# A weight pair in every second attention block, the queries' buffer as a thirteenth weight slot, and two of the eight w_out casts moved into attention

## The chip, the cores and the metric

One core of a Trainium2 chip runs the whole kernel. The metric is device time in microseconds (us). The engines are TensorE (PE in the profile, with its weight loads as PEld), VectorE (DVE), ScalarE (ACT), GpSimd (POOL) and SyncE (SP), whose instruction stream issues nearly all DMA transfers of this kernel. MB and GB/s are decimal; a transfer that the profile shows as 1024.0 KB is 1.049 MB.

## What is computed

The reference is three layers on float32 data, one behind the other:

```python
# 1. chunked attention: 4 batches, 8 heads, 768 tokens, 64 dims; chunks of 32 with 16 left, 8 right
k_full = concat([mem_k, k_ctx]); v_full = concat([mem_v, v_ctx])
scores = scale * (q_c @ k_full.T)
a = exp(scores - max); a = a / (sum(a) + 1e-9); out[:, :, c_start:c_end] = a @ v_full
# 2. soft mixture of experts on x (3072, 512): 8 experts of 4 slots, hidden 1024
logits = x @ phi
d = softmax over tokens; slot_input = d.T @ x
h = maximum(slot_input[e] @ w1[e], 0); slot_out[e] = h @ w2[e]
y = softmax over slots(logits) @ slot_out
# 3. a feed-forward layer on y (3072, 512), hidden 1024
h = y @ w_in; solu = h * softmax(h); ln = layer_norm(solu) * g_ln; result = ln @ w_out
```

`w_in` and `w_out` arrive as float64 (handed over as int64) and are turned into float32 on the chip.

## The kernel before

Every instruction's order is written out by hand. There are three phases.

**Attention**, a loop over 32 blocks (`GROUPS`, index g, lines 780 to 810). One block is a pair of heads, half a sequence, one batch. Per block PE does the score products (`emit_qk`, L245), DVE the softmax (L258 to L271), ACT the exponential and copies, PE a transpose and the value products (`emit_pv`, L292), and then transposes and products for the logits and the slot inputs (L303 to L354). Queries, keys and values come in transfers for two blocks: at an even g, SP issues the queries and keys that are used four blocks later (`load_q` L176, `load_k` L182, two transfers) and, behind `emit_pv(g - 1)`, the values used two blocks later (`load_v`, L182, two transfers). Each has two buffers, so SP holds an issue until PE has read the old content. SP works in order: what is queued behind a held issue waits as well.

In the same SP stream `load_e(LOADS[g])` issues weights ahead of their use. `LOADS` holds 2 at g = 1, 3, 5 of every eight blocks and 0 elsewhere; a 2 stands for 1.049 MB, which is one chunk of `w_in`, two chunks of `w_out`, or one unit of an expert's matrix. The list of what is loaded (`chunks`) is fixed: four times (a `w_in` chunk, two `w_out` chunks), then 32 expert units of 1.049 MB in the order of their use. The `w_out` chunks have places of their own; the others take the first free one of a list of slots. There are eight slots (tiles `e1`, `e2`, named `e_area` in the profile), and a `w_in` slot is freed during its cast. As attention ends, four buffers turn into slots: the two of the keys (`more("kz0")`, `more("kz1")`) and the two of the values; that makes twelve.

A **cast** of a 512-column half chunk (`cast_ops`) is in five steps, one step a block: ACT makes two float copies (L531, L532), DVE does the bits (L535; then L540 and L543), and `eng` multiplies and adds (L546, L549). All eight casts of `w_in` are in attention, with GpSimd as `eng`, starting at blocks `int(3 + 3.4 j)`: 3, 6, 9, 13, 16, 20, 23, 26. The eight casts of `w_out` are in the expert phase with DVE as `eng`, and have two more steps: ACT makes the high part (L566), DVE the low part (L570).

**Experts**, a loop over the 32 units (lines 857 to 874): PE multiplies with a unit (`emit_w1` L447, `emit_w2` L469), frees its slot, and `load_e()` issues the next unit into it (L222). A cast of `w_out` begins at every 2.6th unit (`LANE`), and the steps of the slot softmax (`combine`) run beside them.

**Tail**: 24 tiles of 128 tokens go through the feed-forward layer, planned by a list of times; its main products are L677.

Of the kernel before, what the change touches and what calls it, by code (L numbers as in the profile page):

```python
# [29 lines left out]
DM = H * D  # L30
KC = DM // P
E, SE, FF = 8, 4, 1024
NSLOT = E * SE
FC = FF // P
GT = 3
GROUPS = UNITS * 2
# [2 lines left out]
GREC = GCH + 1  # L39
GTOK = GT * P  # L40
NE = 24
CAST0, CASTN, NEARLY = 3, 3.4, 8
LOADS = [0, 2, 0, 2, 0, 2, 0, 0] * 4
LANE, SIDE = 2.6, 1

CASTU = (0, 1, 2, 3, 4, 5, 6)
C_ID, C_I4, C_REP, C_NM, C_PHI, C_G = 0, 128, 160, 288, 289, 417
# [24 lines left out]
def tile_kernel(ctx: ExitStack, tc: tile.TileContext, qr, kr, vr, w1, w2, w_in, w_out, cst, out):  # L72
# [11 lines left out]
    def area(tag, regions):  # L84

        total = 0
        for name, n in regions:
            total = (total + 31) // 32 * 32
            arenas[name] = [total, n, None]
            total += n  # L90
        tl = sb.tile([P, total], FP32, name=regions[0][0] + "_area", tag=tag)
        for name, _ in regions:
            arenas[name][2] = tl
# [3 lines left out]
    ])  # L97
    for i in range(3):
        area(f"x{i}", [(f"x{i}", GT * DM)])
    area("q", [("q", 4 * GTOK)])  # L100
    for i in range(2):
        area(f"kz{i}", [(f"kz{i}", 2048)])
        area(f"vz{i}", [(f"vz{i}", 4 * VS)])
# [6 lines left out]
    def at(name, off, n, dt=FP32):  # L110
        o, size, tl = arenas[name]
        assert off + n <= size, (name, off, n, size)
        v = tl[:, o + off:o + off + n]
        return v if dt == FP32 else v.bitcast(dt)
# [86 lines left out]
    slot_of = {}  # L201
# [354 lines left out]
        ops = cast_ops(raw(j), at("tmp", 512 * (t % 2), 512), w_in_f[:, sl], eng)  # L556
        return ops[:3] + [lambda: (ops[3](), release(("win", j // 2)) if j % 2 else None)] + ops[4:]

    def wout_ops(j, t):

        w = wo[t % len(wo)]

        def hi():
            area(f"w{j}", [(f"wh{j}", DM), (f"wl{j}", DM)])
            whi[j], wlo[j] = at(f"wh{j}", 0, DM, FP32R), at(f"wl{j}", 0, DM, FP32R)
            act.activation(out=whi[j], in_=w, func=ACTF.Copy, scale=g_sb[:, j:j + 1])  # L566

        return cast_ops(slot_of["wout", j], at("tmp", 512 * (t % 2), 512), w, dve) + [
            hi,
            lambda: dve.scalar_tensor_tensor(  # L570
                out=wlo[j], in0=w, scalar=g_sb[:, j:j + 1], in1=whi[j].bitcast(FP32), op0=ALU.mult, op1=ALU.subtract
            ),
        ]
# [178 lines left out]
    with tc.manual_schedule():  # L752
# [21 lines left out]
        casts = {}  # L774
        early = {}
        for j in range(NEARLY):
            for i in range(5):
                casts.setdefault(int(CAST0 + CASTN * j) + i, []).append((j, i))

        for g in range(GROUPS):  # L780
            if g + 1 < GROUPS:
                emit_qk(g + 1)
            emit_softmax(g + 1)
            if g == GROUPS - 4:
                more("kz0")
            if g == GROUPS - 2:
                more("kz1")
            if g % 2 == 0 and g + 4 < GROUPS:
                load_q(g // 2 + 2)
                load_k(g // 2 + 2)  # L790
            load_e(LOADS[g])
            if 1 <= g:
                emit_pv(g - 1)
            if g % 2 == 0 and 1 < g < GROUPS - 2:
                load_v(g // 2 + 1)
            if g == GROUPS - 2:
                more("vz0")
                load_e()
            for f, hb in todo.get(g, []):
                f(hb)  # L800
            if 3 <= g:
                emit_xt(g - 3)
            emit_t(g)
            emit_at(g)
            if g + 1 < GROUPS:
                emit_exp(g + 1)
            for j, i in casts.get(g, []):
                if j not in early:
                    early[j] = win_ops(j, j)
                early[j][i]()  # L810
        emit_softmax(GROUPS + 1)
        emit_dmax(HB - 2)
# [8 lines left out]
        emit_dt(HB - 2)  # L821
        if not TORD[0]:
            emit_xt(GROUPS - 1, 1)
        more("vz1")
        load_e()
        emit_lg(HB - 1, 3)
# [26 lines left out]
        after = []  # L853
        lane = []
        begun = 0
        waiting = [lambda t, j=j: wout_ops(j, t) for j in range(FC)]
        for n, u in enumerate(units):
            if u == units[-1]:
                keep_clock(bank(5), KEEP[0])
# [134 lines left out]
```

## Time and profile before

| | |
|---|---|
| median of 3 runs | 348.58 us (342.92 to 348.82) |
| the profiled execution | 346.0 us |
| its span in the profile | 344.2 us |
| PE busy | 305.1 us (89%) |
| DVE busy | 233.6 us (68%) |
| ACT busy | 212.4 us (62%) |
| POOL busy | 133.2 us (39%) |
| moved by DMA | 96.62 MB, mean 281 GB/s |

Busy shares are means over three phases with different limits. Attention lasts until about 126 us of the span, the experts until about 184 us, the tail until the end. Times below are microseconds from the span's start. A view by windows gives, for each stretch, what each engine was busy, the TensorE clock that was granted, and what the DMA engines moved.

### The profile page before, as it was taken

The numbers are of one execution on the slowest core, as the hardware profiler recorded it, in microseconds if no ns is written. First come the engines' busy times: TensorE is split into PE (matmuls) and PEld (weight loads), VectorE is DVE, ScalarE is ACT, GpSimd is POOL, SyncE is SP. The second block draws the span as 40 slices with busy tenths as digits, with TensorE's granted clock in tenths as the row PEclk, the third lists the DMA queues.
The fourth block names the chain that finished last, engine by engine and source line by source line (L and its number), as shares of the span: only waits on it lengthen the run. The fifth ranks groups of instructions, "written<-read, shape, count | busy, mean of one in ns | idle before, by whom it ended". The sixth has DMA issues, their size and how long they took to land.

```text
span 344.2 us, 7950 instructions
## 1 busy us (share of the span) xinstructions
PE 305.1 (89%) x3044; PEld 217.0 (63%) x3044; DVE 233.6 (68%) x418; ACT 212.4 (62%) x398; POOL 133.2 (39%) x301
## 2 busy tenths in 40 slices
PE   2796997988989989777757999999999999999996
PEld 2575665666666543332113678888888888888885
DVE  5386685877779359999100796879787878878540
ACT  1254646557566535765112588889888888888721
POOL 5002220231132023332100057777776767676610
PEclk9998999999999999898699999999999999999999
DMA  7989899999899999999990002576766665766631
GB/s 238 388 296 415 296 375 413 342 371 418 310 355 421 421 424 420 421 421 427 420 417 33 2 31 92 184 262 220 235 223 223 222 237 194 243 208 225 231 93 61
DMA packets 31942, 96.62 MB, mean 281 GB/s; under 512 B 4000, under 2 KB 14624, under 8 KB 27296
## 3 DMA queue, kind: packets, MB, share of 16 engines
q1 hardware_dynamic: 31760, 95.90, 74.0%
q8 instruction: 24, 0.39, 0.4%
q10 hardware_dynamic: 144, 0.22, 0.2%
q14 instruction: 14, 0.11, 0.1%
HBM read 79.32 MB, written 16.78 MB: 279 GB/s over the span
## 4 chain that ended last, share of the span: by engine, by line
PE 65%; DMA 23%; DVE 5%; ACT 4%; issue 2%; SPq 1%; ACTq 0%; DVEq 0%
PE bank L677 35%; DMA vz_area<-in_vr_dram 8%; DMA in_kz_area<-in_w_dram 6%; DMA in_vz_area<-in_w_dram 5%; PE bank L292 5%; PE bank L245 4%; DMA kz_area<-in_kr_dram 4%; PE h L589 3%; PE bank L303 2%; PE bank L311 2%; PE bank L317 2%; PE bank L282 2%; PE bank L354 1%; PE bank L447 1%; PE bank L687 1%
## 5 line engine op out<-in xcount | busy, mean ns | idle before, releaser
L677 PE MATMUL bank<-wh_area,yh_area 128*128 128x512 f32 x552 | 130.2, 391 | 0.0
L677 PEld LDWEIGHTS bank<-wh_area,yh_area 128*128 128x128 f32 x552 | 103.4, 188 | 22.1
L546 POOL TENSOR_TENSOR cst_area<-e_area,cst_area 128x512 f32<-128x512 f32 x8 | 10.4, 1305 | 83.1 <-DVE cst_area L258 62.3
L245 PE MATMUL bank<-kz_area,q_area 128*32 128x128 f32 x768 | 30.2, 295 | 10.3 <-DMA kz_area<-in_kr_dram 9.0
L292 PE MATMUL bank<-vz_area,s_area 128*32 128x130 f32 x768 | 29.8, 290 | 8.1 <-DMA vz_area<-in_vr_dram 4.9
L660 DVE STREAM_TRANSPOSE yv_area<-yq_area 128x1024 f32<-128x1024 f32 x20 | 24.9, 1245 | 17.3 <-DMA yq_area<-z 17.3
L604 DVE SCALAR_TENSOR_TENSOR eb_area<-h,eb_area 128x1024 f32<-128x1024 f32 x24 | 29.2, 1220 | 9.4 <-ACT eb_area L598 8.7
L263 DVE TENSOR_REDUCE cst_area<-bank 128x6 f32<-128x384 f32 x32 | 17.8, 557 | 25.9 <-PE bank L245 25.8
L595 DVE TENSOR_REDUCE cst_area<-h 128x1 f32<-128x1024 f32 x24 | 29.1, 1218 | 3.9 <-PE h L589 3.9
L642 POOL TENSOR_SCALAR cst_area<-cst_area 128x1 f32<-128x1 f32 x72 | 28.8, 399 | 7.7
L245 PEld LDWEIGHTS bank<-kz_area,q_area 128*32 128x32 f32 x768 | 21.0, 116 | 16.3 <-issue 6.2
L631 POOL TENSOR_SCALAR cst_area<-cst_area 128x1 f32<-128x1 f32 x24 | 18.5, 770 | 29.9 <-ACT eb_area L598 28.0
L292 PEld LDWEIGHTS bank<-vz_area,s_area 128*32 128x32 f32 x768 | 21.1, 114 | 13.0 <-ACT s_area L285 3.5
L598 ACT ACTIVATE eb_area<-h,cst_area 128x1024 f32<-128x1024 f32 x24 | 26.6, 1110 | 1.3 <-DVE cst_area L595 1.3
L627 ACT ACTIVATE eb_area<-eb_area,cst_area 128x1024 f32<-128x1024 f32 x24 | 27.3, 1139 | 0.1
L624 ACT ACTIVATE eb_area<-eb_area,cst_area 128x1024 f32<-128x1024 f32 x20 | 23.1, 1155 | 5.1 <-DVE eb_area L604 4.7
L671 DVE TENSOR_TENSOR yh_area<-yv_area,yh_area 128x1024 fp32r<-128x1024 f32 x20 | 24.5, 1223 | 2.3 <-ACT yh_area L667 2.3
L306 ACT COPY s_area<-bank 128x384 f32<-128x384 f32 x32 | 15.3, 477 | 15.1 <-PE bank L303 14.8
L667 ACT CAST yh_area<-yv_area 128x1024 fp32r<-128x1024 f32 x20 | 21.0, 1049 | 4.5 <-DVE yv_area L660 4.4
L643 POOL TENSOR_SCALAR cst_area<-cst_area 128x1 f32<-128x1 f32 x72 | 20.3, 283 | 7.1
L695 ACT ACTIVATE eb_area<-bank,cst_area 128x512 f32<-128x512 f32 x23 | 15.8, 686 | 10.3 <-POOL cst_area L633 7.4
L277 ACT ACTIVATE s_area<-s_area 128x384 f32<-128x384 f32 x32 | 16.9, 529 | 6.5 <-DVE s_area L268 6.5
(148 smaller groups left out, 501.3 us busy)
## 6 DMA issues: line engine op xcount, KB each, us to landing
e_area<-in_w_dram SPq DMA_DIRECT2D x23, 1024.0 KB, 13.8
vz_area<-in_vr_dram SPq DMA_DIRECT2D x32, 390.0 KB, 6.9
z<-eb_area SPq DMA_DIRECT2D x20, 512.0 KB, 2.8
yq_area<-z SPq DMA_DIRECT2D x80, 128.0 KB, 3.0
kz_area<-in_kr_dram SPq DMA_DIRECT2D x32, 232.0 KB, 6.3
q_area<-in_qr_dram SPq DMA_DIRECT2D x16, 384.0 KB, 6.3
out_dram<-eb_area SPq DMA_DIRECT2D x23, 256.0 KB, 2.1
in_kz_area<-in_w_dram SPq DMA_DIRECT2D x5, 1024.0 KB, 19.1
```

Of the source, the lines that this page charges most:

```text
L245: pe.matmul(out=bk[32 * j:32 * j + 32, t * 128:(t + 1) * 128], lhsT=qb[g // 2 % 2][:, GTOK * (g % 2) + c * CH:GTOK * (g % 2) + (c + 1) * C ...
L292: pe.matmul(out=bk[32 * j:32 * j + 32, t * 2 * VW:(t + 1) * 2 * VW], lhsT=atb[g % 2][:, c * CH:(c + 1) * CH], rhs=vz[g // 2 % 2][:, :, g % ...
L595: dve.tensor_reduce(out=sc("nm", i), in_=fin["h"][i % 2], axis=AX.X, op=ALU.max, negate=True)
L598: act.activation(out=eb[i % FIN], in_=fin["h"][i % 2], func=ACTF.Exp, bias=sc("nm", i), accum_out=sc("s", i))
L604: dve.scalar_tensor_tensor(out=ub[i % FIN], in0=fin["h"][i % 2], scalar=-1.0 / FF, in1=eb[i % FIN], op0=ALU.mult, op1=ALU.mult, accum_out= ...
L624: act.activation(out=yb[i % FIN], in_=ub[i % FIN], func=ACTF.Identity, scale=-float(FF), bias=sc("nu", i))
L627: act.activation(out=sq, in_=ub[i % FIN], func=ACTF.Square, scale=-float(FF), bias=sc("nu", i), accum_out=sc("vs", i))
L642: pool.tensor_scalar(out=t, in0=r, scalar1=r, scalar2=xx, op0=ALU.mult, op1=ALU.mult)
L660: dve.transpose(out=yv[i % FIN].rearrange("p (f a t) -> p a f t", f=FC, a=4), in_=yq[i % FIN].rearrange("p (a f t) -> p a f t", f=FC, a=4),)
L667: act.copy(out=yh[i % FIN][:, sl], in_=tps(i, sl) if i < NPE else yv[i % FIN])
L671: dve.tensor_tensor(out=yl[i % FIN][:, sl], in0=tps(i, sl) if i < NPE else yv[i % FIN], in1=yh[i % FIN][:, sl].bitcast(FP32), op=ALU.subtract,
L677: pe.matmul(out=fin["o"][i % 2], lhsT=a[i % FIN][:, f * 128:(f + 1) * 128], rhs=w[f], start=start, stop=stop)
```

## The change

The weight table gets its 2 in every odd block, also in g = 7, 15, 23 (and 31). The first block of each cast is given by a table. Two casts of `w_out` (chunks 0 and 1) join the eight of `w_in` in attention, in seven steps from blocks 17 and 24, with GpSimd as `eng`; their result stands in `wo0`, 512 new columns behind the queries' buffer. With these the queries' tile has the size of a slot, and as attention ends it becomes the thirteenth, `in_q`. In the expert phase six casts are left, one begun at every 3.4th unit.

```diff
-CAST0, CASTN, NEARLY = 3, 3.4, 8
-LOADS = [0, 2, 0, 2, 0, 2, 0, 0] * 4
-LANE, SIDE = 2.6, 1
+CASTS = (3, 5, 8, 10, 13, 16, 18, 21, 17, 24)
+NEARLY = len(CASTS)
+LOADS = [0, 2] * 16
+LANE, SIDE = 3.4, 1
...
-    area("q", [("q", 4 * GTOK)])
+    area("q", [("q", 4 * GTOK), ("wo0", DM)])
...
-    def wout_ops(j, t):
-        w = wo[t % len(wo)]
+    def wout_ops(j, t, w, eng=dve):
...
-        return cast_ops(slot_of["wout", j], at("tmp", 512 * (t % 2), 512), w, dve) + [
+        return cast_ops(slot_of["wout", j], at("tmp", 512 * (t % 2), 512), w, eng) + [
...
-            for i in range(5):
-                casts.setdefault(int(CAST0 + CASTN * j) + i, []).append((j, i))
+            for i in range(5 if j < 2 * KC else 7):
+                casts.setdefault(CASTS[j] + i, []).append((j, i))
...
-                    early[j] = win_ops(j, j)
+                    early[j] = win_ops(j, j) if j < 2 * KC else wout_ops(j - 2 * KC, j, at("wo0", 0, DM), pool)
...
+        more("q")
         more("vz1")
         load_e()
...
-        waiting = [lambda t, j=j: wout_ops(j, t) for j in range(FC)]
+        waiting = [lambda t, j=j: wout_ops(j, t, wo[t % len(wo)]) for j in range(NEARLY - 2 * KC, FC)]
```

The first place is on SP, in blocks 4 to 10 of attention (`q_area`, `kz_area`, `vz_area` are the buffers of queries, keys and values). Before, the queue read:

```order
L225 DMA e_area<-in_w_in_dram 128x1024
L176 DMA q_area<-in_qr_dram 128x768
L182 DMA kz_area<-in_kr_dram 64x928 x2
L182 DMA vz_area<-in_vr_dram 64x1560 x2
L176 DMA q_area<-in_qr_dram 128x768
L182 DMA kz_area<-in_kr_dram 64x928 x2
L182 DMA vz_area<-in_vr_dram 64x1560 x2
L225 DMA w_area<-in_w_out_dram 128x512 x2
```

Now it reads:

```order
L227 DMA e_area<-in_w_in_dram 128x1024
L178 DMA q_area<-in_qr_dram 128x768
L184 DMA kz_area<-in_kr_dram 64x928 x2
L184 DMA vz_area<-in_vr_dram 64x1560 x2
L227 DMA w_area<-in_w_out_dram 128x512 x2
L178 DMA q_area<-in_qr_dram 128x768
L184 DMA kz_area<-in_kr_dram 64x928 x2
L184 DMA vz_area<-in_vr_dram 64x1560 x2
```

The two chunks of `w_out` have moved from behind the values of block 8 to behind those of block 6; later weights follow suit, and expert units begin at block 17 in place of 21.

The second place is on SP where attention ends, from the last values (block 28) to the first slots that the expert phase fills again. Before:

```order
L182 DMA vz_area<-in_vr_dram 64x1560 x2
L222 DMA e_area<-in_w_dram 128x2048 x4
L222 DMA in_kz_area<-in_w_dram 128x2048
L222 DMA e_area<-in_w_dram 128x2048
L222 DMA in_kz_area<-in_w_dram 128x2048
L222 DMA in_vz_area<-in_w_dram 128x2048 x2
L222 DMA e_area<-in_w_dram 128x2048 x7
```

Now:

```order
L184 DMA vz_area<-in_vr_dram 64x1560 x2
L224 DMA e_area<-in_w_dram 128x2048 x2
L224 DMA in_kz_area<-in_w_dram 128x2048 x2
L224 DMA in_vz_area<-in_w_dram 128x2048
L224 DMA in_q_area<-in_w_dram 128x2048
L224 DMA in_vz_area<-in_w_dram 128x2048
L224 DMA e_area<-in_w_dram 128x2048 x8
```

Behind the last values nine units were issued before a slot had to be used twice; now there are seven, since six are issued ahead of the last values in place of three. After them 20 units were left, and now 19.

## Rows read from the trace of the kernel before

**Rows 1.** Page: the chain that ended last, shares of the span by engine.

```profile
PE 65%; DMA 23%; DVE 5%; ACT 4%; issue 2%; SPq 1%; ACTq 0%; DVEq 0%
```

**Rows 2.** Windows: stretch, engines' busy us (instructions), clock, DMA share, GB/s.

```profile
24.00:36.00 12.00, 8.60 (x161) 5.99 (x154) 7.02 (x20) 4.83 (x12) 2.58 (x2) 0.86 1.02 412
36.00:46.00 10.00, 9.61 (x218) 7.42 (x219) 7.96 (x22) 7.45 (x20) 2.59 (x2) 1.00 0.85 270
46.00:64.00 18.00, 16.01 (x307) 10.82 (x300) 12.55 (x35) 9.76 (x25) 3.00 (x3) 1.00 1.01 413
64.00:74.00 10.00, 9.06 (x191) 6.63 (x185) 8.26 (x25) 6.36 (x17) 4.13 (x4) 1.00 0.91 322
74.00:90.00 16.00, 14.04 (x263) 9.61 (x260) 11.28 (x33) 9.04 (x24) 3.19 (x3) 1.00 1.02 414
90.00:100.00 10.00, 8.89 (x206) 6.86 (x198) 8.65 (x25) 8.29 (x21) 2.58 (x2) 1.00 0.84 275
100.00:110.00 10.00, 9.95 (x201) 6.93 (x190) 7.62 (x23) 5.32 (x14) 2.58 (x2) 1.00 1.02 418
128.00:146.00 18.00, 14.95 (x174) 6.52 (x165) 17.34 (x32) 11.39 (x26) 6.55 (x7) 0.91 1.01 422
```

**Rows 3.** Timeline of SP in attention: start us, length, line, transfer, count.

```profile
29.32 1.14 SPq L182 DMA_DIRECT2D vz_area<-in_vr_dram  x2
37.13 0.33 SPq L176 DMA_DIRECT2D q_area<-in_qr_dram  x1
```

**Rows 4.** The chain in order of time, 140 to 184: start us, us, what.

```profile
144.65 18.59 DMA in_vz_area<-in_w_dram
...
163.29 19.73 DMA in_kz_area<-in_w_dram
...
183.07 1.06 PE bank L469 x8
```

**Rows 5.** Timeline of SP from the last values to the first refill.

```profile
104.36 1.11 SPq L182 DMA_DIRECT2D vz_area<-in_vr_dram  x2
...
128.06 6.93 SPq L222 DMA_DIRECT2D e_area<-in_w_dram  x7
```

**Rows 6.** Landing times: of those last values (L182, 104 to 106), then of all queries (L176).

```profile
DMA to landing us min/median/max: 5.1/5.3/5.5
...
DMA to landing us min/median/max: 2.9/6.3/8.5
```

**Rows 7.** The chain again: first expert product.

```profile
126.93 2.80 PE bank L447 x48
```

**Rows 8.** Groups by line: casts in attention, then of w_out (busy us, mean ns | idle before).

```profile
L531 ACT ACTIVATE cst_area<-e_area 128x512 f32<-128x512 f32 x8 | 5.5, 682 | 0.0
L532 ACT ACTIVATE e_area<-e_area 128x512 f32<-128x512 uint32 x8 | 5.4, 677 | 0.0
L540 DVE SCALAR_TENSOR_TENSOR cst_area<-e_area,cst_area 128x512 int32<-128x512 int32 x8 | 5.5, 682 | 0.0
L543 DVE TENSOR_SCALAR cst_area<-cst_area 128x512 int32<-128x512 int32 x10 | 4.5, 446 | 0.8
L535 DVE TENSOR_SCALAR cst_area<-cst_area 128x512 int32<-128x512 int32 x10 | 4.2, 417 | 0.0
L546 POOL TENSOR_TENSOR cst_area<-e_area,cst_area 128x512 f32<-128x512 f32 x8 | 10.4, 1305 | 83.1 <-DVE cst_area L258 62.3 <-ACT s_area L277 9.0 <-ACT s_area L306 6.0
L549 POOL TENSOR_TENSOR cst_area<-cst_area 128x512 f32<-128x512 f32 x8 | 10.2, 1277 | 0.6
L566 ACT ACTIVATE wh_area<-wo_area,cst_area 128x512 fp32r<-128x512 f32 x6 | 4.3, 722 | 5.4 <-DVE wo_area L549 5.4
L570 DVE SCALAR_TENSOR_TENSOR wh_area<-wo_area,cst_area,wh_area 128x512 fp32r<-128x512 f32 x6 | 4.5, 744 | 0.9 <-ACT wh_area L566 0.9
```

**Rows 9.** Page: issues of expert units into `e_area`: count, KB each, us to landing.

```profile
e_area<-in_w_dram SPq DMA_DIRECT2D x23, 1024.0 KB, 13.8
```

More of the change, by code (lines that the diff above doesn't have):

```diff
@@ L787, in tile_kernel @@
                 more("kz1")
+                assert max(casts) < GROUPS
             if g % 2 == 0 and g + 4 < GROUPS:
```

## The prediction

> **What bounds the kernel now.** I read the chain of work first: PE holds 65% of it and DMA 23% [rows 1]. In order of time it shows where the DMA part lies. From 144.65 to 183.02 the end is set by two weight loads in a row, 18.59 and 19.73 us, and then by the last expert product [rows 4]. So the expert phase ends when the stream of weights has run out, and whatever brings the last unit in earlier brings the tail earlier by as much. The tail itself is the same in both kernels.
>
> When is the stream out? A view by windows shows how full it is [rows 2]. There are two levels. From 24 to 36, 46 to 64 and 74 to 90 the core moves 412, 413 and 414 GB/s, in the expert phase 422. From 36 to 46, 64 to 74 and 90 to 100 it moves 270, 322 and 275 GB/s. The low stretches come once in eight blocks. The timeline of SP shows what precedes the first: the values of block 6 are issued at 29.32, block 7 has no weight pair, and SP issues nothing until PE has freed the queries' buffer at 37.13 [rows 3]. The loads under way run out, and the next two or three microseconds of issues meet an empty queue. The high stretches are those where each pair of blocks brings a weight pair; queries, keys and values are in them as well, so it is not the kind of transfer that makes the low rate.
>
> **The change part by part.** The baseline is the profiled execution, 346.0 us (span 344.2, and 1.8 around it). It lies 2.6 below the median of the three runs; the mean of these four executions is 346.6, and I state the forecast from that.
>
> *The pairs in blocks 7, 15 and 23.* Every later load moves up by up to three places, so three more expert units, 3 x 1.049 = 3.15 MB [rows 9], come ahead of the last values. The room: against 413 GB/s the three low stretches lack 143, 91 and 138 GB/s over 10 us each, together 3.72 MB [rows 2]. If the new pairs keep the queue from running dry, these stretches rise to 413. Filling all the room is worth 3.72 / 0.413 = 9.0 us, and the three units cost 3.15 / 0.413 = 7.6, so the last values land 1.4 us sooner. If only 3.15 MB of the room is used it is 0; if none, it is 3.15 / 0.370 = 8.5 us later (370 GB/s is the time-weighted mean of the seven windows from 24 to 110). I take -1.4, since the high stretches hold 413 for 18 us on end under the very pattern that the change makes general. PE can follow: it is busy 16.01 us of 18 in that stretch, and 9.95 of 10 where it is not held by loads.
>
> *The expert stream.* Behind the last values 26 units are left in place of 29. At 422 GB/s one takes 1.049 / 0.422 = 2.49 us [rows 2, 9], so three fewer give -7.5 us.
>
> *The hand-over, and the thirteenth slot.* The last values, issued from 104.36, the second transfer some 0.6 later, land 5.3 after that, at about 110.2 [rows 5, 6]. Behind them nine units fill the twelve slots, 9 x 2.49 = 22.4 us, until 132.6, and the first slot is filled again at 128.06 [rows 5]: the stream does not stop. Now only seven units are there, with `in_q` among them: they last 17.4 us. Moved by -1.4 the times are: last values 108.8, stream out at 126.2, first refill issued at 126.7. Until its data flow there is a start-up: 2.9 us is the shortest from issue to landing of 0.393 MB [rows 6], less 0.9 for moving it leaves 2.0, which includes the end of the transfer. So the start-up lies between 0 and 2.0, and the gap between 0.5 and 2.5. I take 1.8. Without `in_q` it would be one unit, 2.5 us, more. After the gap slots come free quicker than loads need them: PE did its first twelve units in 144.65 - 126.93 = 17.7 us, 1.5 each [rows 4, 7], against 2.49 for a load.
>
> *The casts.* One of w_out in attention costs ACT 0.68 + 0.68 + 0.72 = 2.1 us, DVE 0.42 + 0.68 + 0.45 + 0.74 = 2.3 and GpSimd 1.3 + 1.3 = 2.6 [rows 8]; two of them twice that, spread over blocks 17 to 30. I count nothing: in 74 to 90 ACT is busy 9.04 of 16 us and DVE 11.28 [rows 2], and what hides them is that PE waits for loads in every pair of blocks. Without that cover it is up to 2 x (2.1 + 2.3) = 8.8 us. Removing them from the expert phase takes at least 2 x 2.3 = 4.6 us off DVE, busy 17.34 of 18 there [rows 2], and gains nothing by itself, because the stream is what ends last; it only keeps DVE from being late when the phase gets shorter. The earlier starts of the w_in casts cost nothing either, as the chunks they read are also loaded earlier or at the same block.
>
> The sum: -1.4 - 7.5 + 1.8 = -7.1, so 338.9 against the profiled execution and 339.5 against the mean.
>
> One rule speaks against the first step. The Trainium skill (DMA: Bandwidth & Descriptors, Where 436 GB/s comes from) says that between HBM and SBUF the HBM side binds, at some 358 GB/s a core. By that attention would be full already at its mean and nothing could be filled in, which is the first rival below; the high stretches here, at 412 to 422, do not agree with it.
>
> **The rivals.**
>
> *The low stretches stay low on the average, because the queue is limited elsewhere than by missing weights.* Then attention pays 8.5 for the three units and the stream gives back 7.5, with the gap 1.8: +2.8, 349.4. For it: the stretch 90 to 100 stays at 275 although a pair stands in block 25; against it: that stretch begins with the drained queue, and 100 to 110 is back at 418 [rows 2].
>
> *The stream is filled, but PE reaches the expert phase no sooner.* The three units go into the room, and loads queued behind them make queries and values land later, or ACT and DVE are held by the casts near the end. Then the attention term is 0, and each microsecond that PE is late at the first refill lengthens the gap by one. With 0 to 2 us of that: 0 - 7.5 + 1.8 + (0 to 2) gives -5.7 to -3.7, 341 to 343.
>
> *The casts become the bound (slower).* If the 8.8 us of ACT and DVE work stand on the path of the blocks, the first refill comes 8.8 later and the stream stands still meanwhile: -7.1 + 8.8 = +1.7, 348.3. The break-even is 7.1 us of delay, and 2% slower needs 14, one and a half times what the rows give. For it: ACT work waits behind casts in order. Against it: the idle shares above. In a sentence beside it, the Trainium skill (SBUF — State Buffer, Who interferes with whom) says that a DVE instruction with two SBUF inputs and a GpSimd instruction that reads SBUF block each other; the four extra GpSimd instructions would then hold DVE up to 5.2 us, which no row here separates.
>
> *The change does nothing*, if the stream were not what ends last: [rows 4] exclude that for the expert phase. DVE could take over as the bound only if its work there did not shrink, and two of eight casts leave it.
>
> **How the numbers follow.** The forecast has 0.70, with its own range 336 to 342; the second rival 0.15, 341 to 343; the first 0.08, 349 to 351; the casts 0.07, 345 to 354. The predicted time is 339.5. The first two cases hold 0.85 between 336 and 343; with half a microsecond at the lower end for the start-up and three more at the upper one for the spread of single runs (342.92 to 348.82 before) the range is 335.5 to 346. A measurement of this kernel tells about 2% from no change; that bound is 341.6 from the median of the runs shown and 339.1 from the profiled execution. The forecast's middle lies between the two, so of its 0.70 I give 0.50 to faster, and the rest with the second rival and most of the others to the same: faster 0.50, same 0.43, slower 0.07.
>
> **What would show it.** Right, if the windows from 36 to 100 show 400 GB/s and more throughout, the last values land at about 109, the last unit's product starts at about 176 in place of 183.07, and DMA dips for about 2 us around 127. The first step is wrong if a stretch of 8 to 10 us under 330 GB/s is left between 36 and 100. The hand-over is wrong if the dip is over 4 us. The casts are wrong if the chain in attention runs through L531, L532 or L566 for more than a few microseconds, or GpSimd's L546 holds ACT. The forecast as a whole fails if the expert phase ends on something other than a load.

## The result and the profile after

The changed kernel takes 340.31 us in the median of six runs (338.71 to 341.21). The kernel before takes 346.38 in the median of six (342.92 to 350.06). The ratio is 0.9892, with a 95% interval from 0.9855 to 0.9929. It leaves out executions that are more than 1.5% above the fastest of their kernel, and so lies nearer to 1 than the ratio of the two medians, 0.9825. Over all 80 runs of the kernel before that were made beside these experiments the mean is 345.6; over ten of the changed kernel it is 340.7. So the gain is real: 1.1% or 3.7 us by the ratio (its interval says 2.4 to 5.0), 4.9 by the means of all runs. It stays inside 2%. The profiled execution takes 340.69, with a span of 338.9.

The chain that ended last, by engine (page of the changed kernel), with the same DMA share as before and 3 points less of PE [rows 1]:

```profile
PE 62%; DMA 23%; DVE 6%; ACT 5%; issue 1%; SPq 1%; ACTq 0%; DVEq 0%
```

The windows of the changed kernel (stretch, busy us and instructions of PE, PEld, DVE, ACT, POOL; granted clock, DMA share, GB/s), which answer [rows 2]:

```profile
24.00:110.00 86.00, 77.48 (x1488) 55.26 (x1488) 66.74 (x182) 54.85 (x138) 26.38 (x20) 0.98 1.02 404
36.00:46.00 10.00, 7.94 (x163) 5.86 (x166) 7.68 (x21) 7.40 (x18) 3.29 (x4) 1.00 1.00 394
64.00:74.00 10.00, 8.71 (x179) 5.97 (x177) 8.29 (x25) 8.51 (x21) 3.48 (x3) 1.00 1.02 413
90.00:100.00 10.00, 8.82 (x179) 6.56 (x178) 8.58 (x25) 6.38 (x17) 4.45 (x4) 1.00 1.00 390
...
126.00:130.00 4.00, 3.65 (x58) 1.75 (x54) 3.26 (x5) 2.56 (x7) 2.44 (x2) 1.00 0.59 178
128.00:146.00 18.00, 16.41 (x205) 7.40 (x201) 17.52 (x34) 11.80 (x28) 6.70 (x7) 1.00 0.98 406
```

The three low stretches are gone: 394, 413 and 390 GB/s stand where 270, 322 and 275 stood. In their place there is a short dip around 127: 178 GB/s from 126 to 130. It lies at the hand-over from attention to the expert phase, as the timeline of SP shows (start us, length, line, transfer, count; compare [rows 5]), with the landing time of the last values under it (compare [rows 6]):

```profile
103.38 1.11 SPq L184 DMA_DIRECT2D vz_area<-in_vr_dram  x2
...
115.44 0.33 SPq L224 DMA_DIRECT2D in_vz_area<-in_w_dram  x1
126.85 1.19 SPq L224 DMA_DIRECT2D e_area<-in_w_dram  x2
```

```profile
DMA to landing us min/median/max: 5.0/5.4/5.7
```

The last values are two transfers; the second, issued at 103.9, lands 5.7 later, at 109.6. Seven units are issued behind them, the last at 115.44, and then SP issues nothing until PE has freed the first slot at 126.85. Windows cut at that issue show where the dip lies:

```profile
125.00:126.85 1.85, 1.77 (x31) 1.19 (x34) 0.54 (x2) 1.18 (x3) 1.10 (x1) 1.00 0.49 208
126.85:129.00 2.15, 2.04 (x34) 0.96 (x26) 2.12 (x4) 0.71 (x3) 1.53 (x2) 1.00 0.55 99
129.00:130.00 1.00, 0.77 (x8) 0.29 (x12) 0.90 (x2) 1.00 (x4) 0.06 (x1) 1.00 0.98 410
```

The rate falls 1.85 us before the first refill is issued and is back 2.15 us behind the issue. Against 422 GB/s the first window lacks 0.9 us of the stream and the second 1.6, together 2.6.

The chain in order of time (start us, us, what; compare [rows 4]) still ends the expert phase on two loads and the last product:

```profile
139.41 18.51 DMA in_vz_area<-in_w_dram
...
157.99 19.72 DMA e_area<-in_w_dram
...
177.75 1.06 PE bank L471 x8
```

The last expert product starts at 177.75 in place of 183.07, 5.32 us sooner, and the whole execution is 346.0 - 340.69 = 5.31 shorter. So all of the gain is in hand by the last product, and the tail behind it adds nothing in this pair of traces.

### The profile page after: what moved, and what is told of

The parts are those of the page before. It is cut to its first block, busy times and chain, and to the rows that moved or that the text cites. A ratio compares the mean times of both kernels' runs of the same rounds, so it can differ in the third digit from the quotient of the medians.

```text
span 338.9 us, 7947 instructions
## 1 busy us (share of the span) xinstructions
PE 300.3 (89%) x3044; PEld 215.2 (63%) x3044; DVE 230.9 (68%) x414; ACT 212.4 (63%) x398; POOL 131.7 (39%) x305
## 4 chain that ended last, share of the span: by engine, by line
PE 62%; DMA 23%; DVE 6%; ACT 5%; issue 1%; SPq 1%; ACTq 0%; DVEq 0%
PE bank L678 36%; DMA vz_area<-in_vr_dram 9%; DMA e_area<-in_w_dram 6%; DMA in_vz_area<-in_w_dram 5%; PE bank L294 4%; DMA kz_area<-in_kr_dram 4%; PE h L590 4%; PE bank L247 3%; PE bank L305 2%; PE bank L313 2%; PE bank L319 2%; PE bank L356 1%; PE bank L284 1%; PE bank L449 1%; PE bank L688 1%
## 5 line engine op out<-in xcount | busy, mean ns | idle before, releaser
L294 PE MATMUL bank<-vz_area,s_area 128*32 128x130 f32 x768 | 28.8, 281 | 9.8 <-DVE cst_area L545 2.7
L294 PEld LDWEIGHTS bank<-vz_area,s_area 128*32 128x32 f32 x768 | 20.3, 110 | 14.9 <-ACT s_area L287 5.2
L643 POOL TENSOR_SCALAR cst_area<-cst_area 128x1 f32<-128x1 f32 x72 | 26.6, 369 | 7.7
L308 ACT COPY s_area<-bank 128x384 f32<-128x384 f32 x32 | 15.2, 476 | 18.7 <-PE bank L305 18.2
L644 POOL TENSOR_SCALAR cst_area<-cst_area 128x1 f32<-128x1 f32 x72 | 22.7, 315 | 7.1
L287 ACT COPY s_area<-bank 128x384 f32<-128x384 f32 x32 | 15.4, 480 | 4.7 <-PE bank L284 4.7
```

The costliest lines, as they stand in the source:

```text
L294: pe.matmul(out=bk[32 * j:32 * j + 32, t * 2 * VW:(t + 1) * 2 * VW], lhsT=atb[g % 2][:, c * CH:(c + 1) * CH], rhs=vz[g // 2 % 2][:, :, g % ...
L643: pool.tensor_scalar(out=t, in0=r, scalar1=r, scalar2=xx, op0=ALU.mult, op1=ALU.mult)
L644: pool.tensor_scalar(out=r, in0=t, scalar1=1.5, scalar2=r, op0=ALU.add, op1=ALU.mult)
```

## The experiments

The table holds what the runs gave, but for the two kernels of some 432 us, which have their place below. The means are those of all runs. "Landed" is when the second transfer of the last values of attention is in SBUF, "behind" the time from there to the start of the last expert product, both of the profiled execution. With 2.49 us a unit, 26 units take 64.7 us and 29 take 72.2. The experiments ran on four chips, and the kernel before took 345.2 us in the mean beside e1 to e4, 345.1 beside e5 to e7, 346.7 beside e8 to e10 and 346.3 beside e11, so a difference of a microsecond or so between means from two chips shows little.

| run | weight units behind the last values, slots | mean us (runs) | ratio, 95% interval | landed | behind | GB/s, 24 to 110 |
|---|---|---|---|---|---|---|
| kernel before | 29, 12 | 345.6 (80) | 1 | 110.4 | 72.6 | 371 |
| changed kernel | 26, 13 | 340.7 (10) | 0.9892 (0.9855 to 0.9929) | 109.6 | 68.1 | 404 |
| e9_changed_again | 26, 13 | 341.5 (4) | 0.9877 (0.9827 to 0.9928) | 110.2 | 67.9 | 409 |
| e1_loads_only | 26, 12 | 343.9 (10) | 0.9949 (0.9901 to 0.9997) | 110.0 | 71.1 | 412 |
| e2_no_q_slot | 26, 12 | 342.5 (10) | 0.9951 (0.9913 to 0.9989) | 107.6 | 70.9 | 414 |
| e3_old_loads | 29, 13 | 345.1 (10) | 0.9953 (0.9908 to 0.9997) | 107.0 | 72.8 | 378 |
| e4_casts_back | 26, 13 | 341.5 (10) | 0.9920 (0.9871 to 0.9969) | 109.9 | 67.9 | 411 |
| b2_before_again | 29, 12 | 348.8 (1) | none | 108.3 | 73.1 | 375 |
| e5_five_ahead | 27, 13 | 342.1 (10) | 0.9938 (0.9899 to 0.9977) | 108.5 | 71.3 | 396 |
| e6_keep_clock | 26, 13 | 341.0 (6) | 0.9905 (0.9864 to 0.9946) | 109.3 | 68.4 | 411 |
| e7_one_pair | 28, 12 | 343.8 (10) | 0.9986 (0.9955 to 1.0016) | 109.6 | 72.3 | 384 |
| e11_fourteen_apart | 26, 14 | 338.2 (6) | 0.978 (0.9698 to 0.9862) | 106.1 | 65.4 | 412 |

My theory was the prediction's: the expert phase ends when the stream of weights has run out, and the end is the moment of the last values, plus the units behind them, plus whatever time the stream stands still. Its rival was that attention pays for the three units or that PE comes later to the expert phase; the casts were a third suspect.

### One part at a time

The loads alone, on the kernel before:

```diff
-LOADS = [0, 2, 0, 2, 0, 2, 0, 0] * 4
+LOADS = [0, 2] * 16
```

> The kernel before with one edit: the weight pairs also in blocks 7, 15, 23 and 31. Twelve slots, all w_out casts in the expert phase. Stream theory (the end of the expert phase is the end of the weight stream): the windows 36-46, 64-74 and 90-100 rise from 270, 322, 275 to about 390 to 413 GB/s, as with the whole change; behind the last values (landing near 109.5) stand only 6 units, 14.9 us, so the stream stops near 124.5 and starts again near 128: a gap of 3.5 to 5 us in place of about 2. The last unit's product starts at about 180 (177.75 with the whole change, 183.07 before) and the time is about 343. Rival (the casts made the gain): the time stays with the kernel before, 346 or more. Rival (the slot made the gain): the same, 346.

The changed kernel without the queries' buffer as a slot:

```diff
-        more("q")
```

> The changed kernel without the thirteenth slot: the queries' buffer stays unused in the expert phase. Stream theory: one unit less behind the last values, so the gap at the hand-over near 127 grows by one unit's 2.49 us, the last product starts at about 180.2 in place of 177.75, and the time is about 342.8 in place of 340.3. Rival (twelve slots are enough, the gap is only a start-up time): no change, 340.3.

The changed kernel with the old pattern of loads:

```diff
-LOADS = [0, 2] * 16
+LOADS = [0, 2, 0, 2, 0, 2, 0, 0] * 4
```

> The changed kernel with the weight pairs of before (none in blocks 7, 15, 23), so with the slot and the casts alone. Stream theory: the three low stretches are back (near 270, 320, 280 GB/s), the hand-over has no gap since nine or ten units stand behind the last values, and the last product starts at 182 to 183; time 344 to 346. Rival (moving the casts, or the slot, made the gain): near 340 to 341.

Windows of the loads alone, cut at the first refill (issued at 127.74):

```profile
123.00:127.74 4.74, 4.41 (x43) 2.38 (x47) 1.79 (x6) 1.72 (x5) 1.11 (x1) 1.00 0.12 50
127.74:130.50 2.76, 2.41 (x38) 1.11 (x34) 2.55 (x5) 1.30 (x4) 1.58 (x2) 1.00 0.58 166
```

of the changed kernel without the slot (first refill issued at 125.13):

```profile
120.00:125.13 5.13, 4.64 (x46) 2.50 (x50) 2.11 (x7) 1.78 (x6) 1.10 (x1) 1.00 0.20 85
125.13:127.50 2.37, 2.04 (x34) 0.96 (x26) 2.34 (x4) 0.91 (x4) 1.59 (x2) 1.00 0.49 114
```

and of the changed kernel with the old loads, all of attention first:

```profile
24.00:110.00 86.00, 79.24 (x1530) 56.35 (x1530) 68.23 (x188) 55.74 (x140) 26.42 (x20) 0.98 0.98 378
36.00:46.00 10.00, 9.00 (x181) 6.13 (x175) 7.57 (x20) 7.69 (x20) 2.59 (x2) 1.00 1.01 366
...
90.00:100.00 10.00, 9.06 (x195) 6.35 (x183) 7.54 (x21) 6.67 (x18) 2.59 (x2) 1.00 1.00 384
...
126.00:130.00 4.00, 3.87 (x50) 1.66 (x54) 3.79 (x10) 3.12 (x8) 1.50 (x2) 1.00 1.02 430
```

The loads fill attention by themselves: 412 and 414 GB/s in both kernels that have them, 378 in the one that has the slot and the casts alone. With 12 slots, though, six units are left to issue behind the last values where the changed kernel has seven. The stream nearly stands still for some five microseconds before the first refill, at 50 and 85 GB/s, and comes back 2.8 and 2.4 us behind its issue. The time behind the last values is then 71.1 and 70.9 where the changed kernel has 68.1, and 72.6 before. So three microseconds of what the loads could bring are lost without the slot.

The slot without the loads, in turn, has no gap to fill: the stream does not stop (430 GB/s), and 72.6 stays 72.8. Its mean, 345.1, lies with that of the kernel before, and its ratio of 0.9953 says 1.6 us less. One part of what I expected there failed: the mean rate is that of the old loads again, but the three low stretches are not. They have 366, 375 and 384 GB/s in place of about 270, 320 and 280.

In the traces the two parts do not simply add: behind the last values the loads alone bring 1.5 us, the slot alone none, both together 4.5. The times do not separate this from a plain sum: by the ratios the parts bring 1.8 and 1.6 us and the whole 3.7 to 4.2, with intervals of a microsecond and more on each side.

### The casts

The two casts go back to the expert phase, where one is begun at every 2.6th unit again:

```diff
-CASTS = (3, 5, 8, 10, 13, 16, 18, 21, 17, 24)
+CASTS = (3, 5, 8, 10, 13, 16, 18, 21)
-LANE, SIDE = 3.4, 1
+LANE, SIDE = 2.6, 1
```

> The changed kernel with all eight w_out casts in the expert phase again (one begun at every 2.6th unit), weight pairs and thirteenth slot kept. Stream theory: the casts are worth nothing by themselves; the first refill comes up to 1 us sooner since DVE's L571 and ACT's copies leave the end of attention, DVE is busy again through 128 to 162, and the end is still the stream's: last product at 176.5 to 178, time 339 to 340.5. Rival (DVE would be the bound of the shorter expert phase): last product 180 or later, time 342.5 or more.

The mean is 341.5 against 340.7 of the changed kernel, a difference of 0.8 with an uncertainty of about as much. Landed and behind, 109.9 and 67.9, are those of the two traces of the changed kernel (109.6 and 110.2, 68.1 and 67.9). The other pair that differs by the casts, e1 and e2, shows 343.9 against 342.5 in the mean, but the same ratio, 0.9949 and 0.9951, and 71.1 and 70.9 behind. In no trace do the casts move the stream. If they are worth a microsecond it is in a place that I did not find, and that stays open. TensorE's clock is one place to look: its mean over the span is 0.977 in the ten runs of e4 and 0.984 in ten of the changed kernel, though 0.978 and 0.980 in e1 and e2. What they cost is bounded by the chain of the changed kernel in attention, in which these are all the pieces of casts from 36 to 112 (start us, us, line):

```profile
38.28 0.57 ACT cst_area L533
38.85 0.59 ACT e_area L534
...
44.28 0.56 ACT cst_area L533
44.84 0.57 ACT e_area L534
...
92.57 0.59 ACT q_area L533
93.16 0.59 ACT w_area L534
...
109.66 0.67 DVE wh_area L571
```

The first two pairs on ACT are casts of w_in. The third, whose result goes to `q_area`, where `wo0` lies, and the piece of 0.67 us on DVE belong to the moved casts of w_out: 1.85 us of the chain. The last values land no later for it (109.6 and 110.2 with these casts in attention, 109.9 without), so I see no cost; that there is none is not shown by one chain.

### The kernel before once more

> The kernel before, unedited, for a second trace. Theory: the low stretches of the load stream are a property of the order of the loads, so this trace shows them again at 36-46, 64-74 and 90-100, within 15 GB/s of 270, 322 and 275, the last values land at 109.5 to 110.5 and the last product starts at 182 to 183.5. Rival (the first trace was an unlucky execution): the stretches lie 50 GB/s higher or elsewhere, the last values land 2 us sooner or more, and part of the measured gain is the spread of the kernel before.

This failed, and the rival is what came. The last values land at 108.3, 2.1 sooner than in the first trace, the last product starts at 181.39, and the stretches are not where they were:

```profile
24.00:110.00 86.00, 77.80 (x1516) 56.07 (x1520) 64.69 (x179) 52.37 (x133) 20.64 (x16) 0.98 0.97 375
36.00:46.00 10.00, 9.57 (x192) 6.79 (x193) 8.38 (x23) 7.04 (x18) 2.59 (x2) 1.00 0.99 356
64.00:74.00 10.00, 9.07 (x180) 6.43 (x181) 7.53 (x22) 6.27 (x18) 2.59 (x2) 1.00 0.96 349
90.00:100.00 10.00, 9.04 (x187) 6.33 (x180) 7.79 (x22) 6.86 (x19) 2.57 (x2) 1.00 0.94 336
```

356, 349 and 336 GB/s, where [rows 2] have 270, 322 and 275. The mean from 24 to 110 is nearly the same, 375 against 371, and the third trace with the old loads, e3, has 378 with 366, 375 and 384. So how deep the low stretches are, and where their edges lie, belongs to one execution; what comes again is the mean. The 3.72 MB of room that the prediction read from three windows were a reading of one execution; by the means of the three traces, 371 to 378 under 413 over 86 us, the room is 3.6 to 3.0 MB. Three units over 86 us are 3 x 1.049 / 86 = 36.6 GB/s; on 371 to 378 that makes 408 to 415, and the seven traces with all the pairs show 404 to 414. So attention carries three more units in the same time, as far as the scatter lets one tell: the last values land at 107.0 to 110.4 in the three traces with the old loads and at 106.1 to 110.2 in the seven.

### Fewer ahead

If the end is set by the first refill, a unit less ahead of the last values should cost nothing: it would fill the gap. The changed kernel without the pair in block 27:

```diff
-LOADS = [0, 2] * 16
+LOADS = [0, 2] * 13 + [0, 0] + [0, 2] * 2
```

> The changed kernel without the weight pair in block 27: five expert units ahead of the last values in place of six, eight behind them in place of seven. Hand-over theory: the last values land 2.5 us sooner (about 107), the eight units last until about 127, the first refill is issued at 126 to 126.8, so the gap shrinks from 2.8 to between 0 and 1.5 us and the last product starts at 176 to 177; time 338.5 to 339.5. Rival (a pair less leaves a hole in the stream near 100 instead, as in the kernel before): 100-110 falls under 380 GB/s, last product at 177.75 or later, 340 to 341.

A miss: 342.1 in the mean, slower than the changed kernel by about 1.4. The rival had foreseen the hole, though not all of its cost. The missing pair leaves a hole where it was:

```profile
100.00:110.00 10.00, 10.00 (x199) 7.06 (x190) 7.41 (x21) 6.08 (x17) 1.15 (x1) 1.00 0.84 320
...
126.00:130.00 4.00, 3.68 (x55) 2.02 (x54) 2.81 (x5) 2.01 (x6) 2.69 (x2) 1.00 0.91 332
```

320 GB/s over the last 10 us of attention, where the changed kernel has 387 in the same view. The last values meet a queue that is nearly dry, and land sooner after their issue than in the changed kernel (5.0/5.4/5.7 there):

```profile
DMA to landing us min/median/max: 3.3/3.5/3.8
```

One unit more stands behind them, and as there is one more to issue ahead of the first refill, the dip at the hand-over is smaller (332 instead of 178 GB/s). But 71.3 behind is 3.2 more than 68.1, a unit and 0.8: the hole costs more than the smaller dip gives back. The 1.1 us that the values land sooner do not pay for it. I had counted the gap as something that a unit moved behind the values fills at no cost; the unit costs its own 2.49 first.

One pair more than before, in the first of the four gaps alone:

```diff
-LOADS = [0, 2, 0, 2, 0, 2, 0, 0] * 4
+LOADS = [0, 2, 0, 2, 0, 2, 0, 2] + [0, 2, 0, 2, 0, 2, 0, 0] * 3
```

> The kernel before with one more weight pair, in block 7 alone: four units ahead of the last values, eight behind, twelve slots. Stream theory: the first low stretch (36-46) rises to about 400 GB/s, the others stay; eight units last 19.9 us, just as long as the way from the last values to the first refill's data, so no gap or under 1 us; last product 2 to 3.3 us sooner than before (180 to 181), mean time 342 to 343.2. Rival (only the full pattern helps, one pair is swallowed by later stretches): 344.5 to 346.

```profile
36.00:46.00 10.00, 6.90 (x148) 5.35 (x150) 5.81 (x16) 6.11 (x16) 2.56 (x2) 1.00 1.02 417
64.00:74.00 10.00, 8.68 (x180) 6.27 (x178) 7.97 (x24) 6.35 (x17) 3.68 (x3) 1.00 0.92 317
90.00:100.00 10.00, 9.18 (x203) 7.00 (x202) 9.03 (x26) 7.82 (x20) 2.57 (x2) 1.00 0.89 315
```

The pair in block 7 lifts the first stretch to 417 GB/s and leaves the other two at 317 and 315: in this trace the low stretches are where a pair is missing. (That they need not be so low there, e3 has shown.) The time does not follow as I expected. The last product starts at 181.87, not at 180 to 181, and 72.3 behind the last values is only 0.3 less than 72.6, where a unit is worth 2.49; at 126 to 130 there are 358 GB/s, so the stream dips at the hand-over already with eight units. The mean of 343.8 is 1.3 us under that of the kernel before on the same chip; the ratio, 0.9986, shows no gain at all. One unit is at the limit of what ten runs can tell here.

### A fourteenth slot

If the dip at 126 to 130 is the price of a missing slot, a fourteenth removes it. The values' two buffers have room for three units when attention ends. First they were put into one tile and cut anew:

```diff
-        area(f"vz{i}", [(f"vz{i}", 4 * VS)])
+    area("vz", [(f"vz{i}", 4 * VS) for i in range(2)])
...
-        more("vz1")
+        area("vz", [(f"in_vz{i}", 2048) for i in range(3)])
+        free.extend(at(f"in_vz{i}", 0, 2048) for i in range(3))
```

> The changed kernel with a fourteenth slot: the two values' buffers lie in one tile, which gives three slots of 2048 columns when attention ends, in place of two; nothing else is changed. Refill theory (with the new weight pairs the end is set by the first refill: all slots are full by then, and what is left are 32 units less the slots): 18 units are left in place of 19, so the last product starts 2.5 us sooner, at 175 to 175.8 in place of 177.75, and the mean falls from 340.2 to 337.7 to 338.3. Stream theory with a fixed end of attention (last values 109.6 plus 26 units of 2.49 = 174.4, plus some 0.5) gives nearly the same, 175, so more slots would then be worth nothing further. Rival (the three slots wait for the last value products and the stream stops before them, near 120): no gain, 340 to 341.

This failed for a reason that has nothing to do with slots: 432.3 us in the mean, ratio 1.2488 (1.2411 to 1.2566). The group of PE's products with the values says why (line, operation, count | busy us, mean ns | idle before and what ended it), this kernel first and the changed one behind it:

```profile
L294 PE MATMUL bank<-vz_area,s_area 128*32 128x130 f32 x768 | 39.3, 356 | 75.6 <-DMA vz_area<-in_vr_dram 75.0 <-DVE wh_area L571 0.6
```

```profile
L294 PE MATMUL bank<-vz_area,s_area 128*32 128x130 f32 x768 | 28.8, 281 | 9.8 <-DVE cst_area L545 2.7 <-DMA vz_area<-in_vr_dram 2.3 <-ACT s_area L287 2.2
```

PE waits 75.0 us for loads of values, where it waited 2.3. The timelines of SP and PE show for which (start us, length, line, transfer or products):

```profile
32.84 1.18 SPq L184 DMA_DIRECT2D vz_area<-in_vr_dram  x2
...
38.55 1.53 PE L294 MATMUL bank<-vz_area,s_area 128*32 128x130 f32 x24 [5.11 <-DMA vz_area<-in_vr_dram]
```

The values issued at 32.84 are for two blocks later, but the very next products with values start only when these have landed, 5.0 us behind the issue of the second. As both buffers were one tile, the products that read one buffer waited for the load into the other, and the values were no longer double-buffered. The kernel with fourteen slots further below, with a tile for each buffer, has no such wait. The same kernel with the two casts put back has the same flaw and says nothing on the casts (431.8 us, ratio 1.2375):

> The kernel with fourteen slots, but all eight w_out casts in the expert phase (one begun at every 2.6th unit). Refill theory: same first refill within 0.5 us and the same end of the stream, so the same last product as with fourteen slots within 0.7 us and a mean within 0.7 us. Rival (moving the casts is worth 1.3 us by itself, as the means with thirteen slots, 341.5 and 340.2, suggest): mean 1 to 2 us above the kernel with fourteen slots, and the trace shows where: a later last product, or a lower granted clock behind it.

Then the values' buffers kept a tile each, in a pool of their own that is closed when attention ends and followed by one with three slots:

```diff
-        area(f"vz{i}", [(f"vz{i}", 4 * VS)])
+        area(f"vz{i}", [(f"vz{i}", 4 * VS)], vp)
...
-                more("vz0")
...
-        more("vz1")
+        va.close()
+        vq = ctx.enter_context(tc.tile_pool(name="vq", bufs=1))
+        for i in range(3):
+            area(f"v{i}", [(f"in_vz{i}", 2048)], vq)
+            free.append(at(f"in_vz{i}", 0, 2048))
```

> Fourteen slots again, but with the two values' buffers as tiles of their own during attention (so that a load into one waits for nothing of the other), in memory that is given back as a whole when attention ends and cut into three slots. Refill theory: attention as in the changed kernel (last values at 109 to 110, no more than 5 us of PE waiting for values), 18 units left at the first refill in place of 19, last product 2.5 us sooner, at 174.9 to 175.8, and a mean of 337.7 to 338.5 against 340.2 and 341.5 of the changed kernel's two sets of runs. Rival (the end is set by the last values plus 26 units, 174.4, so nothing is left to gain beyond what the start-up after the gap costs): 0 to -1 us, last product 176.7 to 177.7. Rival (three slots that come free only behind the last value products starve the stream between 120 and 126): 340 to 341.5.

It is the fastest version in the mean: 338.2 (333.52 to 342.66), ratio 0.978 with an interval from 0.9698 to 0.9862, which leaves open whether it is 2% faster than the kernel before. Its SP timeline, landing time, windows and chain:

```profile
100.22 1.11 SPq L187 DMA_DIRECT2D vz_area<-in_vr_dram  x2
...
112.29 1.28 SPq L227 DMA_DIRECT2D in_vz_area<-in_w_dram  x3
123.70 3.84 SPq L227 DMA_DIRECT2D e_area<-in_w_dram  x4
```

```profile
DMA to landing us min/median/max: 4.9/5.1/5.3
```

```profile
126.00:130.00 4.00, 3.92 (x50) 1.69 (x54) 3.79 (x10) 3.11 (x9) 1.54 (x2) 1.00 1.00 418
128.00:146.00 18.00, 16.29 (x200) 7.20 (x193) 17.62 (x33) 13.00 (x30) 7.49 (x8) 1.00 1.01 422
```

```profile
152.01 19.45 DMA e_area<-in_w_dram
...
171.51 1.06 PE bank L474 x8
```

Eight units now last from 106.1 to 106.1 + 8 x 2.49 = 126.0, and the first refill is issued at 123.70. The stream does not stop: 418 GB/s at 126 to 130, where the changed kernel has 178, and 65.4 us behind the last values, 0.7 above 26 x 2.49. Against the changed kernel that is 2.7 less behind them; the means differ by 2.5 us with an uncertainty of 1.5, as the six runs lie far apart. That its last values land at 106.1 is not shown to be the slot's doing. The landing ranges from 106.1 to 110.4 over these traces, without regard to slots or casts, and shifts the whole time by as much; the profiled execution was the fastest of the six.

### The changed kernel once more, and its clock

> The changed kernel, unedited, for a second trace and more times on the same chip as the fourteen slots. Both theories: mean 340 to 340.6, last product at 177.3 to 178.2, last values at 109 to 110, a gap in the stream near 127.

The mean is 341.5, 0.9 over what was expected, with four runs from 339.97 to 342.76. The time behind the last values, 67.9 after 68.1, came again to 0.2.

The spread between executions had one more source, the clock that TensorE has as the expert phase ends. From the start of the last expert product to the end of the span the changed kernel and the one before need 161.1 us, the kernel before in its second trace 165.6. Its chain shows the slow stretch, and a window the clock in it (the last column but two):

```profile
181.39 1.77 PE bank L469 x8
...
186.30 3.64 PE bank L496 x16
```

```profile
182.00:190.00 8.00, 7.55 (x35) 3.16 (x27) 0.29 (x1) 1.23 (x3) 0.00 (x0) 0.50 0.00 0
```

L496 takes 3.64 where the changed kernel has 1.92 for the same sixteen products. So I kept PE busier through the end of the phase, with three products that nothing reads behind each of the last ten units:

```diff
             (emit_w1 if u[0] == "w1" else emit_w2)(*u[1:])
+            if n >= 22:
+                keep_clock(bank(5), 3)
```

> The changed kernel with three more products of 512 columns behind each of the last ten expert units (30 in all, into a bank that nothing reads), so that PE is busier while it waits for loads. Clock theory: the differences that the stream does not explain (span less start of the last product: 161.1 with a clock of 1.00 at 176-184, 162.5 and 162.8 us with 0.6 to 0.8) come from TensorE's clock falling to its lower level as PE waits for the last loads; the added products keep it at 1.00 from 150 on, the end behind the last product stays at 161.2 in every execution, and the mean falls by 0 to 0.7 us. Rival: no effect on clock, time 340 to 341; or the added products delay the refills: 341 or more.

The window from 176 to 184 of this kernel, and of the one with the casts back, whose clock fell there:

```profile
176.00:184.00 8.00, 7.15 (x50) 3.26 (x42) 0.29 (x1) 1.73 (x4) 0.00 (x0) 1.00 0.04 14
```

```profile
176.00:184.00 8.00, 7.14 (x42) 2.74 (x34) 0.29 (x1) 0.96 (x3) 0.00 (x0) 0.65 0.03 12
```

The granted clock stays at 1.00 there (from 150 to 160 it is still 0.83), but the mean, 341.0, is that of the changed kernel, and not 0 to 0.7 lower as I had expected. That does not show the clock to be worth nothing there: the added products cost time themselves, as this trace needs 161.7 us from the last product to the end and the changed kernel 161.1 at the same clock. What shows is that holding the clock in this way gains nothing.

## Why the prediction was right, and where it was not

**The time** came out at 340.31, 0.8 above the predicted 339.5 and inside the range. Of the three chances the largest, 0.50, went to a gain of over 2%; what came is less, 1.1% by the ratio and 1.75% by the medians, the case that had 0.43. The sum itself was too large by some 2 us: -7.1 against -5.3 in the two profiled executions and -4.9 in the means. That the time fits better than the sum is luck, and comes from the baseline. The mean of four executions, 346.6, is one above that of eighty, 345.6. With the right baseline the prediction would have been 338.5.

**What bounds the kernel** was right. In every trace the expert phase ends on a load and then the last product.

**The expert stream, -7.5,** was right. With nothing to interrupt it, 29 units take 72.6 and 26 units 65.4 (e11), 7.2 less.

**The pairs in attention, -1.4,** were put too high: -0.8 in the two profiled executions (110.4 to 109.6), and about 0 over all traces, which scatter by more than that. (The 110.2 of the prediction took the median of two landings, 5.3; the second transfer took 5.5.) What failed is the reading "the three low stretches lack 143, 91 and 138 GB/s": I took the depth of one execution's stretches for the kernel's. By the means of three traces the room is 3.0 to 3.6 MB where three units need 3.15, and that gives a term between +0.4 and -1.1. The first rival, that the low stretches stay low and attention pays 8.5, fell: 404 to 414 GB/s in place of 371 to 378. What happened is nearer the first half of the second rival, the attention term of 0; of its second half, PE late at the first refill, nothing came: the refill is issued at 126.85, and I had 126.7.

**The gap of 1.8** was put too low; it is 2.6 to 2.7. Behind the last values the changed kernel needs 68.1, 2.7 more than the kernel whose stream does not stop (65.4), and the windows around 126.85 lack 2.6. The start-up was not the flaw. I had it between 0 and 2.0 and took 1.3; the window behind the issue lacks 1.6, and in the six traces where the stream had nearly run out at the first refill it is 1.5 to 1.8. The step that failed is "stream out at 126.2, first refill issued at 126.7", which leaves 0.5 between them. The same sum with the measured landing, 109.6 + 17.4 = 127.0, would even have the stream last until behind the issue. The rate falls at 125.0 all the same, and 0.9 us are lost before the issue (1.4 in the second trace of the changed kernel). So seven units behind a landing do not keep the queue full for 7 x 2.49 us from that landing. Why not I did not settle; units issued behind the values may be under way already when these are told as landed.

**The thirteenth slot** was put at one unit, 2.5 us. The two kernels with twelve show 71.1 and 70.9 behind instead of 68.1 and 67.9, so it is 3.0 in the traces; in the mean, e2 and the changed kernel differ by 1.8.

**The casts, 0:** no cost was found, with 1.85 us of the chain in attention on them, and at most a microsecond or so that they bring. DVE is still busy 17.52 of 18 us from 128 to 146, and the phase does not end on it.

Together, with measured terms: -0.8 for the last values, -7.2, +2.7, which is -5.3, the difference of the two profiled executions.

## What to carry to other kernels

Where a phase ends when a stream of loads has run out, count two things: when the last load ahead of it has landed plus the bytes behind it, and when the first buffer comes free plus the start-up and the bytes from there; the later one counts. In this kernel more prefetch moved only the first and a further buffer only the second: behind the last values the prefetch alone brought 1.5 us, the buffer alone none, both 4.5, and the next buffer another 2.7. (In the times, by the ratios, each alone is 1.6 to 1.8 and both 3.7 to 4.2.) The bytes behind a landing ran out earlier than their number says, by two microseconds here, so a hand-over that just fits on paper has a gap. The room in low stretches of one trace is not to be added up as a gain: the mean rate over the whole phase, before and after, is what held from one execution to the next.

## What was unexpected in the hardware

A stream of loads that has run out does not come back with the next issue. In the changed kernel the first refill is issued at 126.85; until 129.00 the rate is 99 GB/s and not 422, which is 1.6 us of the stream, and it is 1.5 to 1.8 us in all six traces where the stream had nearly run out. In the changed kernel another 0.9 us were lost before the issue.

TensorE's granted clock was at 0.50 (1.2 of 2.4 GHz) in some executions as the expert phase ended, and at 1.00 in others of the same kernel; in the second trace of the kernel before it fell after 6 us (176 to 182) in which PE was busy 3.11. Over 176 to 184 it was 1.00 in the changed kernel, 0.65 with the two casts put back and 0.85 in the second trace of the kernel before, and the work from the last product to the end took 161.1, 162.8 and 165.6 us. What decides which execution gets which I did not settle. It bears on the comparison: of 74 runs of the kernel before with a clock on record, the 22 with 0.967 or less over the span take 348.2 us in the mean and the other 52 344.5, while ten runs of the changed kernel lie at 0.98 to 0.99. So about 1 us of the 4.9 between the means goes with the clock, and the ratio's 3.7 us is the safer figure for the change in the loads.

Executions of one kernel also differ in when the last values land, by 2.1 us for the kernel before (110.4 and 108.3) though nothing was changed. Single traces shift by as much as the smaller terms of this sum; the time between two events of one trace held to 0.4 us.
